# Running sums in 32-column pieces, clamps replaced by a ScalarE test, one test of the last decays, and a written order for the whole kernel

## The chip, the cores and the metric

The kernel runs on one core of one Trainium2 chip. A core has five engines that work side by side, each through its own queue of instructions: TensorE (PE, matrix products, with its weight loads shown apart as PEld), VectorE (DVE), ScalarE (ACT), GpSimd (POOL) and SyncE (SP), which here only issues transfers. The transfers themselves run on 16 DMA engines. The metric is the device time of one execution in microseconds (us).

## What is computed

Two blocks follow each other. The first is a gated linear recurrence with complex decays, over 4 batches, 8 heads, 768 steps and heads of 48 columns. The second is a feed-forward layer with a SoLU activation and a layer norm on 3,072 rows of 384 columns, 1,024 wide inside.

```python
mag = np.sqrt(a_re * a_re + a_im * a_im)
scale = np.minimum(mag, 0.999) / (mag + 1e-06)
a_re_n, a_im_n = (a_re * scale, a_im * scale)
...
for t in range(S):
    ar, ai = (a_re_n[:, :, t, :, None], a_im_n[:, :, t, :, None])
    new_re = ar * S_re - ai * S_im
    new_im = ar * S_im + ai * S_re
    kv = np.einsum('bhd,bhe->bhde', k[:, :, t], v[:, :, t])
    S_re, S_im = (new_re + kv, new_im)
    y[:, :, t] = np.einsum('bhd,bhde->bhe', q[:, :, t], S_re)
...
h = x @ w_in
h_max = np.max(h, axis=-1, keepdims=True)
e = np.exp(h - h_max)
sm = e / (np.sum(e, axis=-1, keepdims=True) + 1e-09)
solu = h * sm
mu = np.mean(solu, axis=-1, keepdims=True)
var = np.mean((solu - mu) ** 2, axis=-1, keepdims=True)
ln = (solu - mu) / np.sqrt(var + 1e-06) * g_ln
return (ln @ w_out).astype(np.float32)
```

Everything is float32 in and out. `w_in`, `w_out` and `g_ln` reach the kernel beside the attention inputs; the wide weights are stored as 64-bit numbers, which the kernel turns into float32 itself.

## The kernel before

The sequence is cut into 6 pieces of 128 steps; with 4 batches that makes 24 **chunks**, numbered by piece and then by batch. Two neighbouring chunks form a **group**, 12 in all. The kernel is a set of named steps, and a written order says which step comes when; a step issues its instructions on whichever engines it uses, and each engine runs its own instructions in that order. Semaphores make an instruction wait for what it reads or overwrites.

For each group, *prep* steps work on tiles of 128 steps x 768 columns: `clamp` bounds a_re from below (L751, which also leaves the largest value in `seen`) and a_im from both sides (L753); `inverse` (ScalarE, Ln and Exp), `ratio` and `tangent` (DVE, L762 to L768) form the tangent of half the angle, the last of them a clamp to 1.5; `square`, `secant`, `fourth`, `size`, `eps`, `lnm` give the logarithm of the bounded magnitude. `total` (L793) multiplies it by a triangle of ones on PE, which is the running sum over 128 steps; `grow` and `decay` (L797, L800) are its exponentials, `ks` and `qs` multiply k and q by them. `angle`, `on`, `phase` (L847, a running sum of the angles), `nearest`, `part`, `cos` and `sin` give the rotation. `trig` and `exp` load ScalarE's function tables. `last` sends the last row of the decays to 16 partitions, `ends` tests it on DVE and copies it twice side by side on POOL, `turn_ends` and `tot` turn it for the state.

For each chunk, `k2` and `q2` (L906) rotate k and q, `kqb` (L915) transposes 32 x 32 blocks on DVE and `kqt0` (L920) finishes the transpose with four transfers on SP. The first two chunks use `kt`, `qt`, `kT`, `qT` on PE and ScalarE instead. `score0` and `score1` (L962) are the products of k and q, `mask0` (L966) cuts them to a triangle, `values` (L994) multiplies by v and by the state, `carry` and `add` update the state. Then the layer: `turned_x`, `up0`, `up1` (L1035), `exp0` (L1045), `solu0` (L1054), `blocks` and `away` (transpose of z, L1072 and L1077), `spread`, `norm`, `centred`, `down0`, `down1` (L1112), `scale` (L1116) and `store` (L1121). Chunks 0, 1, 2 and 23 transpose z on PE with `zt` and `zT`.

The two weight matrices come in 14 pieces. `fetch` (L685) loads a piece as raw 64-bit words, `raised` rounds the low words in two passes on ScalarE (L692, L694), `convert` (L700 to L704) joins high and low on DVE. Later `again` loads each piece a second time and `inspect` (L707) looks for its smallest magnitude. At the end `verdict` (L1139 to L1152) counts all tests; if one of them fails, a general kernel runs afterwards. With the inputs measured here it does not.

PE works in full width for `total` and `phase` (128 output rows at once), and in four pieces of 32 output rows for `up`, `down`, `carry`, `values` and `score`. The order stands in four strings: START for the first chunks, EVEN and ODD, which are used in turn for chunks 2 to 19 with names relative to the chunk (n) or its group (g), and END.

## Time and profile before

| | us |
|---|---|
| median of 3 runs | 436.76 (435.95 to 441.48) |
| the profiled execution, its time | 441.15 |
| the same, span from first to last instruction | 438.4 |
| busy: PE, DVE, ACT, POOL | 392.0, 361.2, 287.2, 51.7 |
| granted TensorE clock, mean | 0.978 of full |

The profile is one execution. A page line of a group gives the code line, the engine, the operation and its tiles, how often it ran, its busy time and the mean duration in ns, and how long the engine had stood idle before it and for whom. Lines with forty digits cut the span in 40 slices of about 11 us, each digit being the busy share in tenths. The chain of waits goes back from the last instruction, at each step to what released it. "SPq" is SP's queue, in which a transfer is issued; "to landing" counts from there.

Some durations that the prediction uses come from the groups with shapes kept apart. Mean ns of one, 128 partitions each:

| line | operation | columns | mean ns | count |
|---|---|---|---|---|
| L751 | a_re clamp with its accumulated value | 768 / 384 | 942 / 548 | 11 / 2 |
| L753 | a_im clamp | 768 / 384 | 554 / 356 | 11 / 2 |
| L768 | tangent clamp | 768 / 384 | 559 / 360 | 11 / 2 |
| L771, L777 | Square on ScalarE | 768 / 384 | 844 and 831 / 507 | 11 / 2 |
| L774 | Ln with a bias on ScalarE | 768 / 384 | 937 / 600 | 11 / 2 |
| L777 | reading ScalarE's accumulated value | 1 | 189 | 13 |
| L692, L694 | the two passes of `raised` | 512 | 760, 723 | 6 |
| L692, L694 | the same | 384 | 649, 615 | 8 |
| L818, L819 | test of the last decays | 48, on 16 partitions | 167, 191 | 12 |
| L822 | POOL copy of the last decays | 96, on 16 partitions | 592 | 10 |
| L830 | copy of the turned decays | 16, on 96 partitions | 170 | 10 |
| L707 | `inspect` | 512 / 384 | 674 / 561 | 6 / 8 |

Transfers, median us to landing: a raw piece of w_in (512 KB) 6.0, of w_out (384 KB) 5.6; f_kqT (192 KB each, four a chunk) 3.4; f_zT (128 KB each) 3.2; an input of a group (384 KB) 4.8 to 5.2; the last decays (3 KB) 3.7; an output (192 KB) 3.8.

### The profile page before, as it was taken

How to read it: one execution, taken by the hardware profiler on the slowest of the kernel's cores; microseconds unless marked ns; L12 is line 12 of the kernel's file. 1: busy time of each engine (PE TensorE's matmuls, PEld its weight loads, DVE VectorE, ACT ScalarE, POOL GpSimd, SP SyncE). 2: the span in 40 equal slices, each digit the busy share in tenths (PEclk: the TensorE clock that was granted, in tenths of full speed). 3: DMA queues.
4: the chain of work that ended last, by engine and by line, in shares of the span. 5: the costliest groups of instructions: out<-in, count | busy, mean ns of one | idle time of the engine just before them, and what ended most of it. 6: DMA issues, size and time to landing. Idle time of an engine off the chain costs nothing.

```text
span 438.4 us, 15186 instructions
## 1 busy us (share of the span) xinstructions
PE 392.0 (89%) x6590; PEld 220.2 (50%) x6590; DVE 361.2 (82%) x540; ACT 287.2 (65%) x453; POOL 51.7 (12%) x149
## 2 busy tenths in 40 slices
PE   0247858999999989999999999999999999999983
PEld 0025333555655545555554554654655646446861
DVE  4798899989889799799899899899899899753230
ACT  3998995986585685585576667668657757703160
POOL 3000011203001100101011011011021021102010
PEclk9985989999999999999999999999999999999999
DMA  8895808678758868989888878789879674473210
GB/s 222 203 261 160 188 9 184 122 180 179 171 113 192 202 145 200 210 175 221 202 187 203 196 181 207 168 206 223 190 177 204 166 157 107 111 191 85 47 38 29
DMA packets 167771, 72.52 MB, mean 165 GB/s; under 512 B 142224, under 2 KB 155536, under 8 KB 167696
## 3 DMA queue, kind: packets, MB, share of 16 engines
q1 hardware_dynamic: 167552, 71.14, 70.5%
q8 instruction: 54, 0.88, 0.9%
q10 hardware_dynamic: 144, 0.33, 0.3%
q14 instruction: 21, 0.17, 0.1%
HBM read 38.87 MB, written 4.72 MB: 99 GB/s over the span
## 4 chain that ended last, share of the span: by engine, by line
PE 73%; DVE 8%; ACT 8%; DMA 5%; issue 3%; SPq 2%; DVEq 0%
PE f_o L1112 26%; PE f_h L1035 22%; PE f_y L994 8%; PE f_score L962 6%; PE f_phase L847 3%; PE f_L L793 3%; PE f_d L1002 3%; DMA f_kqT<-f_kb 3%; DMA f_raw<-in_moe_w_in_dram 2%; SPq L920 1%; ACT f_bits L692 1%; DVE f_kb L915 1%; ACT f_bits L694 1%; DVE f_z L1054 1%; ACT f_kqT L933 1%
## 5 line engine op out<-in xcount | busy, mean ns | idle before, releaser
L1112 PE MATMUL f_o<-f_w_out,f_zT 128*32 128x384 f32 (+1 forms) x1344 | 132.9, 487 | 0.2 <-ACT f_zT L1067 0.2
L1035 PE MATMUL f_h<-f_w_in,f_xT 128*32 128x512 f32 x1152 | 130.4, 593 | 1.1 <-ACT f_xT L1028 1.1
L1112 PEld LDWEIGHTS f_o<-f_w_out,f_zT 128*32 128x32 f32 (+1 forms) x1344 | 60.8, 113 | 56.1 <-issue 46.0
L1035 PEld LDWEIGHTS f_h<-f_w_in,f_xT 128*32 128x32 f32 x1152 | 46.0, 110 | 63.9 <-issue 58.3
L915 DVE STREAM_TRANSPOSE f_kb<-f_kq 128x1536 f32<-128x1536 f32 x22 | 54.3, 2469 | 2.3 <-DMA f_kqT<-f_kb 2.0
L1054 DVE SCALAR_TENSOR_TENSOR f_z<-f_h,f_z 128x1024 f32<-128x1024 f32 (+1 forms) x36 | 33.9, 978 | 22.7 <-ACT f_z L1045 22.7
L1099 POOL TENSOR_SCALAR f_s<-f_s,f_sum 128x1 f32<-128x1 f32 x24 | 8.3, 348 | 272.2 <-ACT f_z L1093 272.1
L962 PEld LDWEIGHTS f_score<-f_kqT 96*32 96x32 f32 x1536 | 33.0, 112 | 14.5 <-issue 9.9
L1116 ACT ACTIVATE f_ot<-f_o,f_rs 128x384 f32<-128x384 f32 x24 | 14.0, 582 | 39.1 <-issue 18.2
L962 PE MATMUL f_score<-f_kqT 96*32 96x64 f32 (+3 forms) x1536 | 35.5, 239 | 4.4 <-DMA f_kqT<-f_kb 1.9
L1045 ACT ACTIVATE f_z<-f_h 128x1024 f32<-128x1024 f32 x24 | 29.3, 1219 | 13.6 <-PE f_h L1035 13.5
L994 PE MATMUL f_y<-f_att,f_vr 128*32 128x128 f32 x384 | 37.0, 273 | 0.0
L994 PE MATMUL f_y<-f_att,f_v 128*32 128x128 f32 (+1 forms) x384 | 36.6, 273 | 0.0
L793 PE MATMUL f_L<-f_lr,f_mats 128*128 128x384 f32 x48 | 20.0, 541 | 17.3 <-DVE f_lr L788 17.3
L994 PE MATMUL f_y<-f_kqT,f_state 96*32 96x128 f32 (+1 forms) x640 | 34.1, 272 | 0.0
L966 DVE TENSOR_TENSOR f_att<-f_score,f_mats 128x1024 f32<-128x1024 f32 x24 | 29.2, 1216 | 2.4 <-PE f_score L962 2.2
L994 PEld LDWEIGHTS f_y<-f_att,f_v 128*32 128x32 f32 (+1 forms) x384 | 22.6, 103 | 10.4 <-issue 7.7
L1093 ACT ACTIVATE f_z<-f_z,f_less 128x1024 f32<-128x1024 f32 x24 | 27.4, 1142 | 0.0
L847 PE MATMUL f_phase<-f_x,f_mats 128*128 128x384 f32 x48 | 20.5, 549 | 6.8 <-ACT f_x L833 6.8
L850 ACT ACTIVATE f_f<-f_phase,f_bias 128x384 f32<-128x384 f32 x24 | 13.9, 579 | 19.4 <-PE f_phase L847 18.5
L1072 DVE STREAM_TRANSPOSE f_zb<-f_z 128x1024 f32<-128x1024 f32 x20 | 24.7, 1236 | 0.3
L906 DVE TENSOR_TENSOR f_kq<-f_cs,f_k 128x768 f32<-128x768 f32 x24 | 22.8, 952 | 2.0 <-ACT f_cs L864 1.2
(104 smaller groups left out, 616.7 us busy)
## 6 DMA issues: line engine op xcount, KB each, us to landing
f_kqT<-f_kb SPq DMA_DIRECT2D x88, 192.0 KB, 3.4
f_zT<-f_zb SPq DMA_DIRECT2D x80, 128.0 KB, 3.2
f_raw<-in_moe_w_in_dram SPq DMA_DIRECT2D x12, 512.0 KB, 6.0
f_raw<-in_moe_w_out_dram SPq DMA_DIRECT2D x16, 384.0 KB, 5.6
f_ar<-in_a_re_dram SPq DMA_DIRECT2D x12, 384.0 KB, 4.8
f_ai<-in_a_im_dram SPq DMA_DIRECT2D x12, 384.0 KB, 4.9
f_q<-in_q_dram SPq DMA_DIRECT2D x12, 384.0 KB, 5.2
f_k<-in_k_dram SPq DMA_DIRECT2D x12, 384.0 KB, 5.1
```

Of the source, the lines that this page charges most:

```text
L793: nc.tensor.matmul(out=ps, lhsT=tri, rhs=st["lr"][:, i * DM:(i + 1) * DM], start=True, stop=True)
L847: nc.tensor.matmul(out=ps, lhsT=turns, rhs=st["x0"][:, i * DM:(i + 1) * DM], start=True, stop=True)
L915: nc.vector.transpose(out=t, in_=T["kq", c].rearrange("p n h (f j) -> p j (n h) f", j=3))
L962: nc.tensor.matmul(out=scores[r0:r0 + 32, x, r:], lhsT=QK[:, r // 32, x], rhs=QK[:, r // 32:, H + x], start=True, stop=True)
L966: nc.vector.tensor_tensor(out=st["att"].rearrange("p (i u) t -> p i u t", u=2), in0=scores.rearrange("p (i u) t -> p i u t", u=2), in1=mat ...
L994: nc.tensor.matmul(**product)
L1035: nc.tensor.matmul(out=st["h"][r:r + 32, half * 512:(half + 1) * 512], lhsT=st["xT"][:, c * P + r:c * P + r + 32], rhs=w_in[:, c, half * 5 ...
L1045: nc.scalar.activation(out=z, in_=h, func=AF.Exp, accum_out=sums[:, n:n + 1])
L1054: nc.vector.scalar_tensor_tensor(out=z, in0=h, scalar=1.0, in1=z, op0=OP.mult, op1=OP.mult, accum_out=st["sum"][:, 2 + i:3 + i])
L1072: nc.vector.transpose(out=st["zb"], in_=st["z"].rearrange("p (c s f) -> p s c f", s=4, f=32))
L1093: nc.scalar.activation(out=st["z"], in_=st["z"], func=AF.Square, bias=st["less"], accum_out=st["sum"][:, 1:2])
L1112: nc.tensor.matmul(out=st["o"][rows], lhsT=zT, rhs=w_out[:, c], start=(c == 0), stop=(c == KF - 1))
```

## The change

Six things change.

1. `total` and `phase` call a helper that multiplies in four pieces of 32 output rows.
2. `clamp` and the clamp of `tangent` are gone. In their place `sure` takes, on ScalarE, the squared distance of a_re x (1 / a_re) from one, and leaves its sum in `seen`; the verdict asks that it be at most 1e-7.
3. `raised` is one pass, with the rounding left to the conversion to integers on output. Its tile has two buffers instead of three.
4. `last` sends the row of decays into one constant tile, twice where it is turned later. The tests of the twelve groups and the POOL copies are gone; the verdict tests all rows at once. `turn_ends` is a product in three pieces, and `tot` a copy on ScalarE instead of DVE.
5. Tiles are allocated where they are first used, so that the two halves of a pair of steps can come in either order.
6. START, EVEN, ODD and END are replaced by one string that names every step. Nearly all steps stand at other places than before.

```diff
-    rawp, bits = pool("f_raw", 6), pool("f_bits", 3)
+    rawp, bits = pool("f_raw", 6), pool("f_bits", 2)
...
+    rows = const.tile([GH, NG, 2, D], FP, name="f_rows")
...
             y = T["bits", i] = bits.tile([P, NW], I32, tag="bits", name="f_bits")[:, 0:n]
-            nc.scalar.activation(out=y.bitcast(FP), in_=T["raw", i][:, :, 0].bitcast(U32), func=AF.Identity,
-                                 scale=2.0 ** -29, bias=magic)
-            nc.scalar.activation(out=y, in_=y.bitcast(FP), func=AF.Identity, bias=mmagic)
+            nc.scalar.activation(out=y, in_=T["raw", i][:, :, 0].bitcast(U32), func=AF.Copy, scale=2.0 ** -29)
...
-            nc.vector.tensor_scalar(out=ar, in0=ar, scalar1=LEAST, scalar2=None, op0=OP.max, op1=OP.max,
-                                    accum_out=seen[:, 1, o:o + 1])
-            nc.vector.tensor_scalar(out=ai, in0=ai, scalar1=1e15, scalar2=-1e15, op0=OP.min, op1=OP.max)
...
+        def sure(cs, o=g):
+            nc.scalar.activation(out=st["u"][:, cs], in_=st["x0"][:, cs], func=AF.Square, bias=mone,
+                                 accum_out=seen[:, 1, o:o + 1])
+
         def tangent(cs):
             ai, x0 = st["ai"][:, cs], st["x0"][:, cs]
             nc.vector.scalar_tensor_tensor(out=x0, in0=x0, scalar=2.0, in1=ai, op0=OP.subtract, op1=OP.mult)
-            nc.vector.tensor_scalar(out=x0, in0=x0, scalar1=1.5, scalar2=-1.5, op0=OP.min, op1=OP.max)
...
+        def running(ps, i, weights, nm):
+            for r in range(0, P, 32):
+                nc.tensor.matmul(out=ps[r:r + 32], lhsT=weights[:, r:r + 32], rhs=st[nm][:, i * DM:(i + 1) * DM],
+                                 start=True, stop=True)
+
         def total(i):
             ps = st["L", i] = ps_t.tile([P, DM], FP, tag="t", padded_shape=[P, 512], name="f_L")
-            nc.tensor.matmul(out=ps, lhsT=tri, rhs=st["lr"][:, i * DM:(i + 1) * DM], start=True, stop=True)
+            running(ps, i, tri, "lr")
...
         def last():
-            st["ends"] = sml.tile([GH, D], FP, tag="ends", name="f_ends")
-            nc.sync.dma_start(out=st["ends"], in_=st["ar"][P - 1:P, :])
+            for u in range(2 if ti < NC - 1 else 1):
+                nc.sync.dma_start(out=rows[:, g, u], in_=st["ar"][P - 1:P, :])
...
-        def ends():
-            e = st["ends"]
-            ok = sml.tile([GH, D], FP, tag="ok", name="f_ok")
-            nc.vector.tensor_scalar(out=ok, in0=e, scalar1=LEAST, scalar2=None, op0=OP.is_ge)
-            nc.vector.tensor_reduce(out=seen[0:GH, 2, g:g + 1], in_=ok, op=OP.add, axis=AX.X)
-            if ti < NC - 1:
-                e2 = st["e2"] = sml.tile([GH, 2, D], FP, tag="e2", name="f_e2")
-                nc.gpsimd.tensor_copy(out=e2, in_=e.unsqueeze(1).to_broadcast([GH, 2, D]))
-
         def turn_ends():
             ps = st["tot"] = ps_t.tile([P, GH], FP, tag="t", padded_shape=[P, 512], name="f_tot")
-            nc.tensor.transpose(out=ps[0:D2], in_=st["e2"].rearrange("p u d -> p (u d)"), identity=ident[0:GH, 0:GH])
+            ends = rows[:, g].rearrange("p u d -> p (u d)")
+            for r in range(0, D2, 32):
+                nc.tensor.matmul(out=ps[r:r + 32, 0:GH], lhsT=ends[:, r:r + 32], rhs=ident[0:GH, 0:GH], start=True, stop=True)
...
-            nc.vector.tensor_copy(out=T["tot", g], in_=st["tot"][0:D2])
+            nc.scalar.copy(out=T["tot", g], in_=st["tot"][0:D2])
...
-            nc.tensor.matmul(out=ps, lhsT=turns, rhs=st["x0"][:, i * DM:(i + 1) * DM], start=True, stop=True)
+            running(ps, i, turns, "x0")
...
+        nc.vector.memset(row[:, 3:4], 0.0)
+        nc.vector.tensor_scalar(out=ends, in0=rows[:, :, 0], scalar1=LEAST, scalar2=None, op0=OP.is_ge, op1=OP.add,
+                                accum_out=row[0:GH, 3:4])
```

Of the order, the beginning of the old START and of the new string, up to the first `total`, and the part of the new one from chunk 2's scores to chunk 3's:

```diff
-load_ar:0 load_ai:0 clampb:0 clampa:0 inverseb:0 fetch:5 ratiob:0 inversea:0 raised:5 tangentb:0 ratioa:0
-tangenta:0 fetch:9 squareb:0 raised:9 secantb:0 squarea:0 fourthb:0 sizeb:0 secanta:0 convert:9 fetch:0 epsb:0
-sizea:0 fetch:13 lnmb:0 epsa:0 lnma:0 raised:0 fourtha:0 convert:0 convert:5 gain:0 fetch:2 total1:0 decay1:0
...
+load_ar:0 inverseb:0 load_ai:0 ratiob:0 inversea:0 ratioa:0 sureb:0 surea:0 fetch:10 raised:10 tangentb:0 squareb:0
+load_q:0 fetch:1 tangenta:0 squarea:0 secantb:0 secanta:0 sizeb:0 fourthb:0 sizea:0 epsb:0 convert:10 fetch:0 epsa:0
+load_k:0 lnmb:0 fetch:3 raised:0 lnma:0 total1:0 fourtha:0 total0:0 decay1:0 grow1:0 convert:0 grow0:0 fetch:4
...
+qs1:1 up1:1 zT0:0 up0:1 last:1 centre:0 tangent:2 score0:2 square:2 score1:2 centre:3 centre:4 secant:2 centre:5 ks1:1
+exp0:1 size:2 load_k:2 centre:1 centre:6 q2:3 eps:2 load_v:1 fourth:2 k2:3 lnm:2 kqb:3 down0:0 turn_ends:1 tot:1
+total0:2 spread:0 total1:2 grow1:2 grow0:2 mask0:2 decay0:2 decay1:2 trig:2 solu0:1 down1:0 angle:2 load_ar:3 values:2
+kqt0:3 norm:0 scale:0 on:2 load_vr:2 load_ai:3 zt0:1 turned_x:2 zt1:1 carry:2 qs0:2 zT0:1 zT1:1 centred:1 phase0:2
+qs1:2 phase1:2 ks1:2 score1:3 load_v:2 score0:3 up1:2 nearest0:2 nearest1:2 ks0:2 part0:2 load_v:4 part1:2 sin:2 add:2
```

In EVEN stood `again:-4`, `again:-3`, `inspect:-5` and `inspect:-6`, so that the second loads ran through the loop. In the new string the first, `again:12`, stands beside chunk 6; the other thirteen and all `inspect` steps come after chunk 22's scores. The end of the old END and of the new string:

```diff
-up0:23 store:20 up1:23 centred:22 blocks:22 scale:21 away:22 exp0:23 solu0:23 spread:22 down0:22 norm:22
-centred:23 down1:22 zt0:23 zt1:23 scale:22 store:22 zT0:23 spread:23 zT1:23 store:21 down0:23 down1:23 norm:23
-scale:23 store:23
...
+centred:22 store:20 blocks:22 up0:23 scale:21 up1:23 spread:22 away:22 again:2 inspect:5 exp0:23 norm:22 inspect:3
+down0:22 again:0 down1:22 solu0:23 inspect:9 centred:23 scale:22 again:11 again:6 zt0:23 zT0:23 inspect:0 inspect:6
+zt1:23 again:4 again:8 store:22 spread:23 inspect:2 store:21 down0:23 norm:23 inspect:8 again:1 zT1:23 down1:23
+inspect:11 inspect:4 scale:23 store:23 inspect:1
```

## The prediction

> **What bounds the kernel now.** I read the page first, then windows along the span, then the chain of waits, then the queues in the places the chain points to.
>
> ```profile
> PE 392.0 (89%) x6590; PEld 220.2 (50%) x6590; DVE 361.2 (82%) x540; ACT 287.2 (65%) x453; POOL 51.7 (12%) x149
> ...
> PE   0247858999999989999999999999999999999983
> ...
> DVE  4798899989889799799899899899899899753230
> ```
>
> TensorE (PE) is saturated from about the seventh slice (11 us each) to the last but one; before that DVE is the full one. So there are three stages: a fill that PE waits through, a loop, a drain.
>
> ```profile
> 22.00:33.00 11.00, 5.06 (x13) 2.44 (x14) 10.53 (x22) 10.59 (x19) 0.44 (x1) 0.87 0.95 262
> ...
> 55.00:66.00 11.00, 6.41 (x102) 3.52 (x102) 10.21 (x25) 10.23 (x18) 1.47 (x4) 0.84 0.04 8
> ...
> 153.50:186.60 33.10, 31.68 (x591) 17.21 (x594) 29.55 (x40) 21.31 (x33) 3.36 (x11) 1.00 0.80 186
> 186.60:217.80 31.20, 31.20 (x588) 17.15 (x588) 29.21 (x40) 21.17 (x33) 4.08 (x11) 1.00 0.89 203
> ...
> 425.00:438.40 13.40, 6.04 (x23) 3.29 (x21) 0.46 (x3) 2.86 (x5) 1.33 (x5) 0.92 0.16 53
> ```
>
> A row gives the stretch, its length, then busy us by engine. In the fill PE works 5 to 9 of 11 us and DVE 10.2 to 10.5: **DVE bounds the fill**. In the loop one pair of chunks takes 31.2 to 31.3 us with PE busy throughout and DVE at 29.2: **PE bounds the loop**. One pair takes 33.1, with 1.4 us of idle PE.
>
> ```profile
> 63.28 0.87 DVE f_ar L751 x2
> 64.14 0.47 DVE f_ai L753
> ...
> 67.35 2.29 DVE f_kb L915
> ...
> 71.65 3.97 DMA f_kqT<-f_kb
> 75.76 1.28 PE f_score L962 x34
> ...
> 302.80 1.49 PE f_L L793 x4
> ...
> 310.16 1.51 PE f_phase L847 x4
> ...
> 319.39 5.16 PE f_o L1112 x64
> ```
>
> This is the chain that ended last (start, length, what). The clamps of L751/L753 stand on it in front of the block transpose of chunk 2 (f_kb); its transfer lands and chunk 2's scores start at 75.76. From there the chain is nearly all matmuls back to back. L793 and L847, the running sums, take 1.49 and 1.51 us a pair; the 64 pieces of f_o take 5.16, that is 0.645 us for each 384-column product over all 128 rows (8 of them).
>
> ```profile
> 169.46 2.86 SPq L685 DMA_DIRECT2D f_raw<-in_moe_w_in_dram  x1
> ...
> 172.84 3.08 SPq L868 DMA_DIRECT2D f_on<-f_f  x1
> 176.02 3.51 SPq L920 DMA_DIRECT2D f_kqT<-f_kb  x4
> ```
>
> SP's queue in the slow pair: the re-read of a weight (L685) holds the queue 2.86 us, f_on another 3.08, and only then the next chunk's transpose leaves. PE's scores wait for it until 183.5.
>
> ```profile
> 425.73 5.43 PE L1112 MATMUL f_o<-f_w_out,f_zT 128*128 128x384 f32 x16 [0.24 <-ACT f_zT L1067]
> ...
> 431.33 0.58 ACT L1116 ACTIVATE f_ot<-f_o,f_rs 128x384 f32<-128x384 f32 x1 [3.96 <-PE f_count L1149]
> 431.50 0.14 DVE L1152 TENSOR_SCALAR flag<-f_total 1x1 int32<-1x1 f32 x1
> ```
>
> The end: the last matmuls stop at 431.16, the flag is written at 431.64, and 6.8 us later the span ends. Flag and last store are equally late here.
>
> **The Trainium skill.** "TensorEngine Tiling (Array Packing)", Key Properties: column tiles run independently, and a change of tiling mode drains the array. The trace agrees in size: a full-width pair costs 1.49 us between 32-column neighbours, against 2 x 0.645 = 1.29 for pieces. "ScalarE: Activation LUTs", What ACT_TABLE_LOAD costs: 280 ns + 0.833 ns an element with a pointer bias, so an estimate of 920 ns for 768 elements; L774 with such a bias took 937, L777 without 831. "DMA: Bandwidth & Descriptors", Queues, rings and completion order: each DMA engine takes descriptors of a ring in order, so a small transfer stands behind large ones issued before it on SP; the 3.08 us of f_on behind the weight agrees.
>
> **The change, part by part** (changes of time; minus is a gain).
>
> 1. *Running sums.* 48 full-width products (12 groups, two of L793, two of L847) become 192 pieces. A group goes from 1.49 + 1.51 to 4 x 0.645 = 2.58, so -0.42. Groups 2 to 11 lie where PE bounds: **-4.2**. Groups 0 and 1 lie in the fill and count there. Bounds: 0 if the drain remains in another form, -5 for all twelve.
>
> 2. *Clamps and end tests on DVE.* Removed up to the end of chunk 2's transpose at 69.6: L751 0.548 x 2 + 0.942 x 2 with 0.08 each to read the sum, L753 0.356 x 2 + 0.554 x 2, L768 0.36 x 2 + 0.559, the end test 0.17 + 0.19, f_tot 0.17; 6.9 us together. 2.7 of it is group 0's, in the first 13 us, where DVE idles for loads and ScalarE anyway. **4.2 us** lie in the stretch DVE fills. In the loop DVE loses 1.58 + 0.56 + 0.36 + 0.17 = 2.7 a pair; that shortens nothing on PE by itself, but removes what made the slow pair late.
>
> 3. *ScalarE.* "raised" loses its second pass: 8 x 0.615 + 6 x 0.723 = 9.3 us, all in the fill. The test "sure" adds 0.60 x 2 + 0.19 x 2 for group 0 and 0.94 + 0.19 for each later group, f_tot about 0.2 (no such copy on ScalarE shown; between DVE's 0.17 and the 0.47 of a 384-column copy). To 69.6 that is 9.3 - 4.2 = 5.1 us less. Group 0 gains directly: Ln starts on the landed a_re instead of behind a clamp, and the first running sum's exponentials need no longer follow a two-pass "raised". Walking the written order with these durations, I put decay1 of group 0 near 17.2 instead of 19.69. The new waits: tangent (DVE) now waits for "sure" (ScalarE), because both use f_x; behind tangent on DVE stand conversions, kq products and masks, for which PE waits in turn. "raised" with two f_bits buffers instead of three waits for a conversion (1.5 to 1.9 us), with exp and the copies of kqT behind it.
>
> Parts 2 and 3 with the new order give **-6** for the start of chunk 2's scores, 75.8 to about 69.7: 4.2 from the DVE stretch, about 2 from the earlier start. PE has the same work ahead of that point in both orders (two chunks through up, chunk 0's z turned). Bounds: -1 (each saved DVE op turns into a wait for ScalarE or a load) and -8.
>
> 4. *Order in the loop.* 13 of the 14 re-reads (again) leave the loop for the drain, so the 2.86 us holds on SP go, and with the lighter DVE the idle 1.4 us of the slow pair and 1 us between 77 and 122. New: chunk 3's scores come ahead of chunk 2's up, with only 12 us of PE work to cover DVE's about 14 before its transpose lands; I charge 1. Input loads are spread singly instead of in clusters; up to ten more 3 KB row transfers (second copy of the last decays) cost 0.55 each on SP and replace a POOL copy of 0.59. Net **-1.5**. Bounds: -3 and +8 (nearly 1 us of idle PE a pair; a new order isn't in this trace, so a loss is not excluded).
>
> 5. *The drain.* 13 re-reads of 384 or 512 KB and all 14 reductions (0.56 or 0.67) now follow chunk 22's scores. DMA was at 22% in 400 to 425, so most fit. The last ones don't: weight 8 waits in its buffer for the reduction of weight 9, which stands behind chunk 23's solu on DVE (done 6.9 before PE's end); weight 1 comes after two stores and the reduction of weight 2, about 4.4 before PE's end. With the row's median landing of 6.0 it lands 1 to 2 after PE's end; reduction 0.67, verdict 0.95 and the count follow, and the flag comes 2.5 later than now. **+2.3**; bounds 0 (DMA nearly empty there, landing in 3 us) and +4.5.
>
> 6. *At nothing:* constants and memsets (0.06 each, under the first load), one verdict test less, an added zero fill.
>
> Sum: -4.2 - 6 - 1.5 + 2.3 = **-9.4 us**. The profiled execution took 441.15 us with a span of 438.4, 4.4 above the median of 436.76; I move the difference over unscaled: 436.76 - 9.4 = **427.4**.
>
> **Rivals.**
> - *The gain stays in the fill or is spent in the drain (change within 2%).* For it: DVE and ScalarE alternate in the fill, so a shorter op can become a wait (ScalarE idles 4.54 us at 69 to 74 for f_x); the late re-read. Against: DVE idles under 1.3 us in each slice from 22 to 66. Then -4.2 - 2 + 0.5 + 3 = -2.7: about 434.
> - *The loop gets a new bound (slower).* Mechanism: each group's tangent holds DVE until "sure" comes up on ScalarE behind an exp of h that itself waits for PE; mask and transpose stand behind it. A pair leaves DVE 30.8 - 25.4 = 5.4 us of slack (29.2 less 2.7 and less about 1.1 of reductions moved out). It passes 2% slower when it eats all the gain and 8.7 more, 18.1 over ten groups, that is when the hold is over 5.4 + 1.8 = 7.2 us in every group. For 9 us of hold: 427.4 + 10 x 3.6 = 463. Against: ScalarE is busy only 21.2 of 31.3.
> - *Pieces are no faster than whole products.* Then the sum is -5.2: 431.6. Against it stand f_o and f_h, which run in just such pieces.
>
> **Numbers.** Forecast 0.70: three quarters of it under 428.0. Within-2% rivals together 0.18. New bound 0.07. Fill better than walked and the late re-read hidden, 0.05: near 421. A measurement of this kernel tells about 2% (8.7 us) from no change. Faster by over 2%: 0.52 + 0.05 = 0.57; slower 0.07; the rest, 0.36, within. The forecast alone spans 421 to 433; the range 419 to 436 also takes in most of the small-gain rivals, and leaves out the new bound and some of the tails.
>
> **What would show it.** L793 and L847 as 128*32 rows near 0.32 us of chain per four records; no DVE rows for the clamps; chunk 2's scores near 69.7; pairs near 30.8 us with PE full; the last reduction after PE's last matmul and the flag near 2.5 us behind PE's end. I am wrong if chunk 2's scores start after 74, if pairs exceed 31.3, or if PE's waits name "sure", f_kqT or f_x in the loop.

## The result, and the profile after

| | before | after |
|---|---|---|
| median, first set (20 runs each) | 437.57 | 433.74 |
| ratio, 95% interval | | 0.990 (0.9874 to 0.9926) |
| median, second set (35 and 6 runs) | 438.45 | 433.07 |
| ratio | | 0.986 (0.9816 to 0.9901) |
| median, third set (19 and 6 runs) | 439.07 | 434.57 |
| ratio | | 0.990 (0.9862 to 0.9935) |
| profiled execution, its time and span | 441.15, 438.4 | 432.79, 430.9 |

The ratios are formed from single runs, without one slow run of the changed kernel, and are not exactly the quotients of these medians.

The change makes the kernel 3.8 to 5.4 us faster; forecast were 9.4. The two profiles that lie beside each other differ by 7.5 us of span, nearly twice the medians: the profile of before was a long execution, that of after a short one. This matters below.

From the page of the changed kernel, busy time by engine, then the slices of PE and DVE:

```profile
PE 383.9 (89%) x6928; PEld 207.5 (48%) x6928; DVE 336.9 (78%) x457; ACT 287.7 (67%) x475; POOL 57.6 (13%) x139
...
PE   0258677999999999999998999999999999999990
...
DVE  3789988997798798599788699789787888872352
```

PE has 8 us less to do than before and DVE 24 less; in the loop DVE's slices now stand mostly at 7 to 9. The same kernel in windows (stretch, length, then busy us and instructions of PE, PEld, DVE, ACT, POOL, then granted clock, DMA share and GB/s): two slices of the fill, an undisturbed pair of chunks, a stretch of a little over a pair in the middle, and the end.

```profile
22.00:33.00 11.00, 5.87 (x32) 3.08 (x24) 9.88 (x17) 9.62 (x17) 0.00 (x0) 1.00 1.02 247
55.00:66.00 11.00, 7.54 (x58) 3.21 (x58) 8.23 (x12) 6.57 (x11) 0.00 (x0) 0.84 0.39 66
115.05:145.72 30.67, 30.67 (x620) 16.01 (x616) 24.93 (x29) 22.23 (x37) 5.08 (x13) 1.00 0.73 167
205.35:239.66 34.31, 32.95 (x682) 18.90 (x678) 27.55 (x32) 22.12 (x36) 5.16 (x14) 1.00 0.81 172
418.00:430.90 12.90, 3.06 (x11) 1.44 (x9) 4.14 (x17) 0.58 (x1) 0.00 (x0) 0.81 0.22 81
```

At 55 to 66 DVE works only 8.2 and ACT 6.6 of 11 us: the fill is no longer DVE's there. A pair takes 30.67 instead of 31.27 with PE full and DVE at 24.9. At 205 to 240 PE stands idle for 1.36 us.

What the scores of chunk 2 now wait for, in ScalarE's and then TensorE's timeline (start, length, what; in brackets how long the engine had stood idle and for whom):

```profile
62.05 0.48 ACT L765 COPY f_meanp<-f_parts 128x384 f32<-128x384 f32 x1 [4.37 <-PE f_parts L760]
62.55 1.28 ACT L936 ACT_TABLE_LOAD   x1
63.84 0.58 ACT L1107 COPY f_zT<-f_zt 128x512 f32<-128x512 f32 x1
64.32 0.85 ACT L798 ACTIVATE f_lr<-f_ar 128x768 f32<-128x768 f32 x1
65.20 0.84 ACT L799 ACTIVATE f_x<-f_lr 128x768 f32<-128x768 f32 x1
65.95 0.46 ACT L1068 COPY f_xT<-f_y 128x384 f32<-128x384 f32 x1
```

```profile
56.97 2.46 PE L760 MATMUL f_parts<-f_w_out,f_gs 128*32 128x384 f32 x8 [2.26 <-DVE f_gs L757]
...
60.40 1.59 PE L760 MATMUL f_parts<-f_w_out,f_gs 128*32 128x384 f32 x8
...
66.47 5.36 PE L1075 MATMUL f_h<-f_w_in,f_xT 128*32 128x512 f32 x48 [1.37 <-ACT f_xT L1068]
71.64 1.31 PE L1001 MATMUL f_score<-f_kqT 96*32 96x128 f32 x64
74.53 2.82 PE L1152 MATMUL f_o<-f_w_out,f_zT 128*128 128x384 f32 x8 [1.57 <-DVE f_w_out L770]
```

DVE finished the block transpose of chunk 2 at 62.78; in the kernel before it was 69.63, so the forecast gain of 6 us would have put it near 63.6. But the scores start at 71.64, because chunk 1's h is ahead of them on PE, and its input f_xT is copied by ScalarE behind the mean of w_out, a table load and group 2's two passes of `inverse`. After the scores f_o waits another 1.57 for the centred w_out.

And the end, in DVE's timeline: the last re-read's reduction, and the flag. PE's last product ends at 420.87.

```profile
418.30 1.60 DVE L749 TENSOR_REDUCE f_least<-f_raw 128x1 f32<-128x384 f32 x3 [2.55 <-DMA f_raw<-in_moe_w_out_dram]
420.79 0.69 DVE L749 TENSOR_REDUCE f_least<-f_raw 128x1 f32<-128x512 f32 x1 [0.88 <-DMA f_raw<-in_moe_w_in_dram]
...
423.67 0.14 DVE L1195 TENSOR_SCALAR flag<-f_total 1x1 int32<-1x1 f32 x1
```

The flag comes 2.9 us behind PE's end; forecast were 2.5.

### The profile page after: what moved, and what is told of

Same layout as the page of the kernel before. It is cut to its first block, busy times and chain, and to the rows that moved or that the text cites. A ratio compares the mean times of both kernels' runs of the same rounds, so it can differ in the third digit from the quotient of the medians.

```text
span 430.9 us, 15839 instructions
## 1 busy us (share of the span) xinstructions
PE 383.9 (89%) x6928; PEld 207.5 (48%) x6928; DVE 336.9 (78%) x457; ACT 287.7 (67%) x475; POOL 57.6 (13%) x139
## 4 chain that ended last, share of the span: by engine, by line
PE 69%; DVE 11%; ACT 7%; DMA 5%; SPq 3%; issue 3%; DVEq 0%; ACTq 0%
PE f_o L1152 24%; PE f_h L1075 22%; PE f_y L1034 8%; PE f_score L1001 4%; PE f_phase L838 3%; PE f_L L838 3%; PE f_d L1042 2%; DMA f_v<-in_v_dram 2%; DVE f_kq L947 2%; DVE f_kb L956 1%; DMA f_ar<-in_a_re_dram 1%; DMA f_raw<-in_moe_w_in_dram 1%; SPq L1117 1%; PE f_parts L760 1%; DMA out_dram<-f_ot 1%
## 5 line engine op out<-in xcount | busy, mean ns | idle before, releaser
L1152 PE MATMUL f_o<-f_w_out,f_zT 128*32 128x384 f32 (+1 forms) x1344 | 130.2, 487 | 3.0 <-DVE f_w_out L770 1.6
L1075 PEld LDWEIGHTS f_h<-f_w_in,f_xT 128*32 128x32 f32 x1152 | 42.1, 110 | 65.4 <-issue 61.4
L956 DVE STREAM_TRANSPOSE f_kb<-f_kq 128x1536 f32<-128x1536 f32 x22 | 57.4, 2609 | 2.7 <-DMA f_kqT<-f_kb 2.4
L1139 POOL TENSOR_SCALAR f_s<-f_s,f_sum 128x1 f32<-128x1 f32 x24 | 12.0, 502 | 173.8 <-ACT f_z L1133 173.7
L838 PE MATMUL f_L<-f_lr,f_mats 128*32 128x384 f32 x192 | 19.3, 517 | 17.4 <-DVE f_lr L833 17.4
L1001 PE MATMUL f_score<-f_kqT 96*32 96x64 f32 (+3 forms) x1536 | 33.0, 234 | 1.0 <-ACT f_kqT L974 1.0
L893 DVE SCALAR_TENSOR_TENSOR f_f<-f_f,f_phase 128x384 f32<-128x384 f32 x24 | 12.9, 553 | 21.3 <-ACT f_f L889 21.0
L1130 POOL TENSOR_SCALAR f_less<-f_sum 128x1 f32<-128x1 f32 x24 | 10.8, 448 | 123.5 <-DVE f_z L1094 123.1
L947 DVE TENSOR_TENSOR f_kq<-f_cs,f_q 128x768 f32<-128x768 f32 x24 | 22.8, 950 | 5.0 <-ACT f_cs L902 4.0
L1156 ACT ACTIVATE f_ot<-f_o,f_rs 128x384 f32<-128x384 f32 x24 | 13.6, 568 | 19.4 <-PE f_o L1152 13.5
L1068 ACT COPY f_xT<-f_y 128x384 f32<-128x384 f32 x24 | 11.2, 469 | 22.6 <-PE f_y L1034 22.6
```

The lines of the kernel that those rows point to most:

```text
L838: nc.tensor.matmul(out=ps[r:r + 32], lhsT=weights[:, r:r + 32], rhs=st[nm][:, i * DM:(i + 1) * DM], start=True, stop=True)
L947: nc.vector.tensor_tensor(out=t, in0=T["cs", g][:, i * H:(i + 1) * H], in1=heads(T[nm, g][:, i]).unsqueeze(2).to_broadcast([P, H, 2, D]), ...
L956: nc.vector.transpose(out=t, in_=T["kq", c].rearrange("p n h (f j) -> p j (n h) f", j=3))
L1001: nc.tensor.matmul(out=scores[r0:r0 + 32, x, r:], lhsT=QK[:, r // 32, x], rhs=QK[:, r // 32:, H + x], start=True, stop=True)
L1075: nc.tensor.matmul(out=st["h"][r:r + 32, half * 512:(half + 1) * 512], lhsT=st["xT"][:, c * P + r:c * P + r + 32], rhs=w_in[:, c, half * 5 ...
L1152: nc.tensor.matmul(out=st["o"][rows], lhsT=zT, rhs=w_out[:, c], start=(c == 0), stop=(c == KF - 1))
```

## The experiments

Comparisons are with the kernel before, run beside it on the same chip. "Scores" is the start of chunk 2's scores, "middle" from there to the end of PE's last f_o, "tail" from there to the end of the span.

### e1: the kernel before again

No edit.

> The kernel before, unchanged, profiled once more. Theory A (the profiled execution that the forecast was built on was itself long: 441.15 against a median of 437.57 over 20): this execution has a span near 435, and the 3 us less are missing at a few places of the fill or as waits of PE in the loop (the pair of 33.1 us at 153 to 186 is then near 31.3, chunk 2's scores start earlier than 75.8). Theory B (the executions all look like that one and the time outside the span differs): span near 438, chunk 2's scores near 75.8, a pair of 33 us again. Ratio 1.00 in both.

Measured: 438.16 us, ratio 0.998 (0.9963 to 1.0006); span 436.6, scores 76.02, middle 353.1 (355.4 in the first profile), tail 7.5. The pair of 33.1 us is not there: all pairs between 121 and 340 take 31.27. So about 2 us of the profile that I predicted from belonged to that one execution, and the gain that I booked for "the slow pair" could not be counted on in a median. What I had read as its cause is in e1 as well: the re-read and f_on hold SP's queue for 2.58 and 2.94 us at 169 to 175, and PE idles only 0.2 us in the whole loop. In the first profile the two waits of PE in the slow pair were these:

```profile
PE f_d L1002 <- issue: 1.2, 1, 1.2
PE f_score L962 <- DMA f_kqT<-f_kb: 0.2, 1, 0.2
```

The longer one stands ahead of f_d at 154.2 to 155.4, 14 us before those holds, and the profile names nothing that it waited for. Only the 0.2 us are a wait for the transpose.

### e2: the running sums in pieces, alone

The kernel before with `running` in `total` and `phase`, nothing else.

```diff
-            nc.tensor.matmul(out=ps, lhsT=tri, rhs=st["lr"][:, i * DM:(i + 1) * DM], start=True, stop=True)
+            running(ps, i, tri, "lr")
```

> The kernel before with only the running sums in four pieces of 32 rows, in the old order. If the term of the forecast holds: pairs of 30.8 instead of 31.3, 10 pairs, so -4 to -5 us, ratio 0.989 to 0.991. Rival (DVE, at 29 of 31 us a pair, takes over as the bound, so that the faster sums turn into waits for the transposes): -1 to -2 us, ratio 0.995 to 0.998, with PE idle in the pairs.

Measured: 435.06 us, ratio 0.9935 (0.9913 to 0.9958), that is -2.8 us. The chain of an undisturbed pair by line, first of e1 (246.52 to 277.79), then of e2 (243.24 to 273.88):

```profile
by line: PE f_o L1112 33.5%; PE f_h L1035 33.0%; PE f_y L994 11.3%; PE f_score L962 7.6%; PE f_phase L847 4.8%; PE f_L L793 4.8%; PE f_d L1002 4.6%; PE f_tot L826 0.5%
```

```profile
by line: PE f_h L1040 33.8%; PE f_o L1117 33.8%; PE f_y L999 11.5%; PE f_score L967 7.5%; PE f_phase L793 4.4%; PE f_d L1007 4.3%; PE f_L L793 4.2%; PE f_tot L831 0.6%
```

Of 31.27 and 30.64 us these are: f_L 1.49 and 1.29, f_phase 1.51 and 1.35, and also f_o 10.46 and 10.34, f_d 1.43 and 1.31, f_score 2.38 and 2.30. The products' own rows give 0.36 of the 0.63 us; the rest is in their neighbours in 32-column mode, most plainly in f_d. **A pair gains 0.63 us, not 0.42.** Ten pairs would give 6.3, an estimate; in the old order PE then idles 2.0 us between 93 and 403 (0.2 in e1), and one pair takes 31.58 without any wait, so that less arrives, 2.8 by the medians.

### e3: all edits in the code, the old order

The changed kernel with the old order; `sure` directly after `ratio`, and some conversions moved up for the two f_bits buffers. Around group 3, for example:

```diff
-clamp:3 ... ratio:3 up0:3 tangent:3
+ratio:3 sure:3 up0:3 tangent:3
```

> All code edits of the change, but the old order: clamps and end tests left out, the test on ScalarE put right after ratio, and five conversions of weights moved ahead so that two buffers are enough. If the written order is what spends the gain: ratio under 0.985 (-6.5 us or more: sums -4.5, lighter DVE and ScalarE in the fill -3 to -6, no cost at the end, flag as before about 7 us from the last product to the end of the span). If the written order is itself what brings the earlier chunk 2: ratio 0.988 to 0.995, chunk 2's scores near 74 to 76, and the tail again near 7.2 us.

Measured: 450.64 us, ratio 1.025 (1.021 to 1.030): **slower by 12 us** by the medians (438.5 before). Scores at 80.9. What DVE and, between 85 and 420, PE waited for (us in total, times, longest):

```profile
DVE f_x L816 <- ACT f_u L811: 13.5, 13, 1.5
```

```profile
PE f_score L1004 <- DMA f_kqT<-f_kb: 4.6, 6, 1.5
PE f_d L1045 <- issue: 3.4, 2, 2.6
```

L816 is `tangent`, L811 `sure`: the hold of my rival "the loop gets a new bound" is there, about 1.1 us a group instead of the 7.2 from which it decides. In the changed kernel's own order the same wait is 0.3 us in all. That this hold makes mask and transpose late, and so PE's waits for f_kqT, is likely, but no run shows it alone. In the fill it is something else: the transpose of chunk 2 ends at 69.7, as in e1 (69.9), and the 4.9 us by which the scores come later stand on PE ahead of chunk 1's h:

```profile
73.55 7.56 PE L1078 MATMUL f_h<-f_w_in,f_xT 128*32 128x512 f32 x48 [4.77 <-ACT f_xT L1071]
```

Here `sure` of group 2, put directly after `ratio`, waits on ScalarE for DVE, and the copy of x for chunk 1 stands behind it. The 7.56 us are a product at half clock for the most part (5.36 in the changed kernel). So the 12 us belong to all the edits with `sure` at this place; another place in the old order was not tried, and the running sums alone pay in it (e2).

### e4: the re-reads in the loop, in the new order

The changed kernel with its 14 `again` and `inspect` steps spread over groups 2 to 11, as in EVEN, for group 4:

```diff
-secant:4 load_vr:3
+secant:4 again:4 load_vr:3
...
-lnm:4 score0:6
+lnm:4 inspect:3 score0:6
```

> The changed kernel with the 14 second loads and their reductions put back through the loop (two a pair, ended by group 9), the rest of its order as it is. If the tail costs what its trace shows: from PE's last product to the end of the span 7.2 instead of 10.0 us, so -2.5 to -3 us against the changed kernel, ratio to before near 0.983. Rival (the loads hold SP's queue and DMA in the loop as before): the tail shrinks by 2.8 but the pairs grow by 0.3 or more, ratio 0.988 to 0.993.

Measured: 435.56 us, ratio 0.9933 (0.99 to 0.9966). The flag comes 0.48 behind PE's end, but the middle is 354.3 in this profile. The executions fall in two groups, 433.3 to 434.7 with a mean granted clock of 0.98 to 0.993, and 435.6 to 438.8 with 0.973 to 0.978; the profile is of the second. So the re-reads in the loop are no gain on the whole, and may be no loss either.

### e5 and e13: the changed kernel again

No edit.

> The changed kernel again, unaltered. If its first profile stands for it, the span is 430 to 433 us, chunk 2's scores start at 71 to 72.5 and the pairs take 30.5 to 30.9. If that execution was a lucky one, the way my base execution was an unlucky one, the loop shows it: more than 352 us from chunk 2's scores to TensorE's last matmul (349.2 in the first profile), and a ratio to the kernel before of 0.992 or more.

> The changed kernel, unaltered, as the base of this call. 432.5 to 434 us as in the two calls before; chunk 2's scores at 71.2 to 72.5, and the pairs of groups 6 and 8 longer than 30.7 by 1 to 2 us together.

Measured: 433.07 and 434.57 us. Against e1, in us:

| | e1 | after | e5 | e13 |
|---|---|---|---|---|
| scores | 76.02 | 71.64 | 71.88 | 71.83 |
| middle | 353.1 | 349.2 | 349.9 | 351.4 |
| tail | 7.5 | 10.0 | 12.6 | 12.3 |
| span | 436.6 | 430.9 | 434.4 | 435.5 |

In these three the start of the scores repeats within 0.3, but that is luck: kernels with the same order up to there have it at 71.2 to 73.5 (e4, e8, e10), and e12 and e14, one kernel, at 73.1 and 69.6. The first profile was short in its tail and middle; those of e5 and e13 are the slowest of their six executions. What PE waited for in e5 between 85 and 420:

```profile
PE f_y L1034 <- DMA f_v<-in_v_dram: 0.6, 1, 0.6
PE f_o L1152 <- ACT f_ot L1156: 0.6, 1, 0.6
PE f_h L1075 <- ACT f_xT L1068: 0.3, 1, 0.3
PE f_o L1152 <- ACT f_zT L1107: 0.3, 1, 0.3
```

Between 93 and 403 PE idles 1.6 to 1.9 us in the three profiles, e1 0.2. The new order costs idle time in the loop where I had booked a gain.

### e6: full-width sums in the new order

```diff
-            running(ps, i, tri, "lr")
+            nc.tensor.matmul(out=ps, lhsT=tri, rhs=st["lr"][:, i * DM:(i + 1) * DM], start=True, stop=True)
```

and the same for `turns`.

> The changed kernel with the running sums as full-width products again. If the pieces are worth in the new order what they were alone in the old one (-2.8 us) or what I forecast (-4.2), this kernel is 2.8 to 4.2 us slower than the changed one, close to the kernel before (ratio 0.997 to 1.0), and pairs take 31.0 to 31.3. If the saving is covered in the new order by waits for other engines, it is under 1.5 us slower.

Measured: 439.79 us, 6.7 above e5 beside it; ratio to before 1.002 (0.9991 to 1.0045). **Without the pieces the whole change is worth nothing.** Its scores start 4.2 us earlier than in e1, but the middle is 1.8 and the tail 4.1 us longer: the gain of the fill is spent behind it. The window of an undisturbed pair of e6:

```profile
146.86:178.13 31.27, 31.27 (x594) 16.08 (x590) 26.10 (x32) 22.09 (x36) 3.73 (x10) 1.00 0.76 157
```

31.27 again, as in the old order, with DVE 3 us lighter: a lighter DVE does nothing for a pair in which PE is full.

### e7 and e16: the fill in another order

e7 is the changed kernel with chunk 1's turned_x ahead of inverse:2 and three centre steps ahead of ratio:2.

```diff
-load_q:3 centre:2 values:1 zT1:0 inverse:2 ratio:2 kqt0:2 centre:7 onward:1 turned_x:1 sure:2
+load_q:3 centre:2 centre:7 centre:0 centre:3 values:1 zT1:0 turned_x:1 inverse:2 ratio:2 kqt0:2 onward:1 sure:2
```

> The changed kernel with chunk 1's turned_x ahead of group 2's inverse on ScalarE, and three of the eight centre steps ahead of group 2's ratio on VectorE. If what kept chunk 2's scores at 71.6 instead of 69.7 is the place of these steps in the written order, the scores start near 70.1, the product f_o after them no longer waits 1.6 us for f_w_out, and the time falls by 1.5 to 3 us against the changed kernel. If the fill is bound elsewhere (the two Exp/Ln passes of group 2 now come 0.5 later, and its tangent with them), the scores move but the time stays within 0.7 us.

Measured: 435.88 us, 2.8 more than e5. Scores at 72.2; up:1 no longer waits for f_xT, but f_o waits longer. PE's timeline at f_o, and windows of e7:

```profile
76.69 3.54 PE L1154 MATMUL f_o<-f_w_out,f_zT 128*128 128x384 f32 x5 [3.16 <-DVE f_w_out L772]
```

```profile
70.00:76.00 6.00, 3.53 (x88) 1.83 (x80) 5.01 (x9) 4.78 (x6) 0.00 (x0) 0.99 0.88 142
76.00:82.00 6.00, 5.31 (x8) 2.52 (x8) 6.00 (x7) 2.93 (x6) 0.00 (x0) 0.50 0.45 60
```

In the 3.2 us of idle PE the clock (third number from the end) falls to 0.50, from 75.8 to 82.7. The Trainium skill, "TensorE: Matmul & The Clock Gate", What's actually happening, says that after an idle window of about 3.4 us, which runs freely, TensorE falls to half rate. The traces agree in kind: each profile of before and after shows half clock somewhere in the fill, for 3.4 us or a multiple of it, and not at the same place in every execution (e1 at 77.3 to 80.7, the first profile of before not there). They differ in one thing: PE need not have idled for all of such a window. In the 3.4 us ahead of these stretches it had idled 1.9 us in e1, 2.3 in e5 and 2.3 in e7. e16 puts repeated products into that gap:

```diff
+            if (c, half) == (2, 1):
+                xs += [0, 1, 2, 3, 4, 5, 6, 7, 0, 1, 2, 3, 4, 5, 6, 7]
+            for x in xs:
```

> The kernel of e7 (turned_x and three centre steps earlier) with all sixteen half-head products of chunk 2's scores formed twice more right after score1:2, about 2.6 us of additional work for TensorE where it idled 3.16 us before f_o and then ran at half clock for six us (74 to 82). If that half clock is what made e7 2.8 us slower than the changed kernel, this kernel has full clock from 74 on and is 2 to 3 us faster than e7's 435.9, near the changed kernel. If not, it is as slow as e7 or slower by the additional work.

Measured: 434.73 us, ratio 0.990 (0.9868 to 0.9936; e7: 0.995, 0.9924 to 0.997, so that the two are only nearly apart); the changed kernel beside it, e13, 434.57. The same two windows of e16:

```profile
70.00:76.00 6.00, 5.10 (x194) 4.33 (x185) 5.63 (x10) 5.74 (x7) 0.00 (x0) 1.00 1.16 176
76.00:82.00 6.00, 6.00 (x58) 2.95 (x60) 6.00 (x10) 5.09 (x11) 1.05 (x3) 1.00 0.25 54
```

The clock stays at 1.00, and the scores start at 69.7, where I had forecast them. Both need care, for e7's profile is the slowest of its 22 executions and e16's the fastest of its 6. Up to the scores the two kernels are the same, and yet e7 has them at 72.2. From the start of f_mean to the scores it takes 7.7 us in both and 9.1 in after and e13: the wait for f_xT was worth 1.3 us, and the rest of e16's early start belongs to its execution. For the clock the other executions speak too: its mean is over 0.984 in none of e7's 22, but in 3 of 6 of e16, 5 of 6 of e5 and 4 of 6 of e13. So work that nobody needs probably removed the half clock. But the total is no better than the changed kernel's: the scores start 2.1 earlier than in e13, the extra products take 2.3, and f_o starts at 74.2 instead of 74.7.

### e15: the same for the gap ahead of the mean

The changed kernel with chunk 1's scores formed once more, and half of them twice more, behind score0:1.

```diff
+            if (c, half) == (1, 0):
+                xs += [4, 5, 6, 7, 0, 1, 2, 3, 4, 5, 6, 7]
```

> The changed kernel with twelve head products of chunk 1's scores formed a second time right after score0:1, the same values into the same place: about 2 us of additional work for TensorE at 54.7 to 56.7, where it idled 2.3 us before the first product of the mean and then ran at half clock. If the idle stretch is what halves the clock, the products of the mean run at full clock (about 1.45 us for each eight instead of 2.46 and 1.59), and chunk 2's scores start no later or up to 1.5 us earlier, though TensorE has 2 us more to do. If the clock falls for another reason, the additional work only adds: scores 0 to 0.5 later, the mean still at half clock.

Measured: 437.63 us, ratio 0.997 (0.9944 to 0.9994), 3 us slower than e13. The clock had already halved at 52.5, behind 2.25 us of idle time ahead of f_phase, so the filler ran slowly; and e13 without it has the mean at full clock as well (1.45 and 1.48). The scores start at 71.74, as in e13. This run tells nothing on the cause. Its loss is in the loop, where PE idles 3.1 us between 93 and 403; why the filler should do that there I can't say.

### e8: the re-reads two places earlier in the drain

Of the end of the order (the first two stand beside chunks 20 and 21):

```diff
-scale:22 again:11 again:6 zt0:23 zT0:23 inspect:0 inspect:6 zt1:23 again:4 again:8 store:22
+scale:22 again:4 again:8 zt0:23 zT0:23 inspect:11 inspect:6 zt1:23 again:1 store:22
```

> The changed kernel with thirteen re-reads and their reductions two places earlier in the drain, each in the place that the one two before it had, the first two beside chunks 20 and 21. If the flag is late only because the last re-read lands late, it comes 0.5 to 1 us behind TensorE's last matmul instead of 2.9, and the time falls by 2 to 2.5 us. If the DMA engines or VectorE's queue are what is full at the end, TensorE ends later by about what the flag gains and the time stays within 0.7 us.

Measured: 432.14 us, 0.9 less than e5, ratio 0.9846 (0.9799 to 0.9893). The flag comes 0.48 behind PE's end, as expected, 3.2 earlier than in e5; but from flag to span end it takes 9.4 us, in the kernel before 6.8. This led to e11.

### e9: the clamps on VectorE in the new order

`clamp` of the kernel before directly ahead of each inverse, the clamp of `tangent` back, no `sure`; the verdict's bound on `seen` is the old one.

```diff
-inverse:3 spread:1 down1:1 turned_x:3 ratio:3 exp0:2 sure:3 solu0:2 kqt0:4 tangent:3
+clamp:3 inverse:3 spread:1 down1:1 turned_x:3 ratio:3 exp0:2 solu0:2 kqt0:4 tangent:3
```

> The changed kernel, order and all, with the three clamps of a group on VectorE again and no ScalarE test. My forecast's term 2 says VectorE's 4.2 us ahead of chunk 2's transpose come back: the transpose ends near 68.5 instead of 64.7, chunk 2's scores start 2 to 4 us later, the loop's pairs stay at 30.7, and the time rises by 3 to 4 us. The rival: in the new order the fill waits for TensorE (the mean of w_out) and ScalarE, so that VectorE's work is hidden, and the time rises by under 1 us; or the clamps also delay the ratio in the loop behind late input loads, and it rises by over 5.

Measured: 460.83 us, ratio 1.053 (1.048 to 1.058), some 27 us above the changed kernel of the other sets: the rival, and far beyond its bound. Waits of DVE, then of PE between 85 and 420:

```profile
DVE f_ar L811 <- DMA f_ar<-in_a_re_dram: 6.5, 3, 3.4
...
DVE f_ai L813 <- DMA f_ai<-in_a_im_dram: 3.3, 4, 1.4
```

```profile
PE f_h L1080 <- DVE f_z L1099: 7.5, 6, 2.0
PE f_zt L1107 <- DVE f_z L1099: 3.7, 2, 3.4
```

At that place DVE waits up to 3.4 us for an input, and solu and the transpose of z stand behind it. So this run gives no price of the clamps; it shows that they can't be put back at this place of the new order, whose loads of a_re come too late for a reader on DVE there. The transpose of chunk 2 ended 2.0 us later than in e5, not 3.8, and the scores started 5.9 us later.

### e10, e11, e12 and e14: three losses taken out

e10 moves two loads of group 7 up.

```diff
-part0:6 nearest1:6 ks0:6 qs1:6 away:9 part1:6 scale:8 onward:6 score0:11 carry:10 sin:6 add:10 cos:6 exp:6 load_ai:7 ks1:6 load_ar:7
+part0:6 load_ar:7 nearest1:6 ks0:6 qs1:6 away:9 part1:6 load_ai:7 scale:8 onward:6 score0:11 carry:10 sin:6 add:10 cos:6 exp:6 ks1:6
```

> The changed kernel with load_ar:7 and load_ai:7 moved ahead of nearest1:6 and scale:8, as far ahead of their inverse as the loads of the groups before and after stand. If the 1.4 us of idle TensorE between 220 and 242 come from a_re of group 7 landing 7 us after its issue, just when its Ln is due, with chunk 11's turned_x queued behind on ScalarE, the two pairs there together take 61.4 instead of 63 and the time falls by 1.2 to 1.8 us. If the store's landing at 232 alone holds TensorE, only 0.6 to 0.8 us goes.

Measured: 433.86 us, ratio 0.9897 (0.9864 to 0.9931), the same as the changed kernel. The wait for the store is gone, but PE now waits 0.9 us for f_zT at 294 and 0.5 at 212: the loss moved.

e11 sends the last decays once and lets POOL make the second copy.

```diff
-            for u in range(2 if ti < NC - 1 else 1):
-                nc.sync.dma_start(out=rows[:, g, u], in_=st["ar"][P - 1:P, :])
+            nc.sync.dma_start(out=rows[:, g, 0], in_=st["ar"][P - 1:P, :])
+
+        def ends():
+            nc.gpsimd.tensor_copy(out=rows[:, g, 1], in_=rows[:, g, 0])
```

> The changed kernel with one transfer of the last decays a group, the second copy made on POOL as in the kernel before: ten transfers fewer in SP's queue. In the changed kernel SP's closing sequence has one pause of 2.0 to 2.4 us (in one profile 1.1) between two of its instructions, in the kernel before none, and it stands at another instruction wherever the count of SP's instructions differs. If the pause belongs to a place in SP's instruction stream that the longer queue has moved into the end, it is gone: flag to span end near 6.8 us instead of 7.1 to 9.4, and the time falls by up to 2 us. If it belongs to the reads outstanding at the end, it stays and the time is the same within 0.7 us.

Measured: 432.69 us, ratio 0.9895 (0.9861 to 0.9929); by the time alone not to be told from the changed kernel. By the trace the first theory holds: no pause, and 6.4 us from flag to span end. Counting SP's recorded instructions shows where the pause stands (the longest gap in its closing sequence behind the branch, from start to start; the count starts at 0):

```
kernel           SP instructions   longest gap       ahead of number
before, e1, e2         470         0.43              469 (its last)
e11                    466         0.43              465 (its last)
e12, e14               465         0.43              464 (its last)
e4                     474         2.12              472
e8                     476         2.31              472
after, e5, e13         477         1.15, 2.33, 2.22  472
e6, e7, e9             477         2.31, 2.11, 2.29  472
e10, e15, e16          477         2.66, 1.30, 0.84  472
e3                     480         2.42              472
```

In all 12 profiles with more than 472 instructions on SP the pause lies ahead of number 472, whatever that instruction is. A block of instructions that is fetched late would look like this; that it is one was not shown. The last packets of the kind "instruction" ahead of SP's going on end 0.3 to 2.5 us before it, so the trace doesn't settle it. The kernel before ends three short of it.

e12 and e14 are one kernel, with the edits of e8, e10 and e11.

> The re-reads two places earlier, the loads of group 7 earlier and one row transfer a group, together. If the three are separate losses: 2.0 (flag at 0.5 instead of 2.9 behind TensorE's end, of which 0.9 was measured alone) + 1.4 + 2.0 = about 3.5 to 5 us less than the changed kernel, near 429. If they overlap or a moved load delays another transfer, the time stays at 431 to 433.

> The combined kernel again, beside the changed one on the same chip. If its three edits are separate losses of the changed kernel (tail 2.4, SP's pause 0 to 2.3, group 7's loads 0.5 to 1), it is 2 to 4 us faster than the changed kernel in this call and under 0.985 of the kernel before. If its 430.4 was a draw of the executions, the two come out within 1 us.

Measured: 430.42 us, ratio 0.9819 (0.9776 to 0.9862), and 430.10, ratio 0.9808 (0.9775 to 0.9841), in the second case 4.5 us less than e13 beside it. PE's waits between 85 and 420 and the end on DVE, of e14:

```profile
PE f_o L1158 <- ACT f_zT L1113: 0.3, 1, 0.3
PE f_y L1040 <- DVE f_k L866: 0.2, 1, 0.2
PE f_d L1048 <- ACT f_xT L1074: 0.2, 1, 0.2
```

```profile
410.70 3.27 DVE L751 TENSOR_REDUCE f_least<-f_raw 128x1 f32<-128x512 f32 x6
...
418.39 0.14 DVE L1201 TENSOR_SCALAR flag<-f_total 1x1 int32<-1x1 f32 x1
```

PE idles 0.55 us between 93 and 403, all reductions are done 4 us before PE's end, and the tail is 7.3 us as before the change. This profile is the fastest of its seven executions, but by the medians too this kernel beats both.

## Why the prediction was wrong

Right in direction, and the measured time lies in the range; wrong in size by about half. The terms of its sum beside what the profiles showed:

| term | forecast | e1 to after | e1 to e5 | e1 to e13 |
|---|---|---|---|---|
| running sums | -4.2 | -6.3 | -6.3 | -6.3 |
| scores of chunk 2 | -6 | -4.4 | -4.1 | -4.2 |
| written order | -1.5 | +2.5 | +3.1 | +4.6 |
| drain, tail | +2.3 | +2.6 | +5.1 | +4.8 |
| sum | -9.4 | -5.6 | -2.2 | -1.1 |

The row of the sums is an estimate, 0.63 x 10 pairs; the row of the written order is the change of the middle less these. 1.6 us of it is f_o's wait behind the scores, 1.4 to 1.7 are additional idle time of PE in the loop. These are single executions; the medians changed by -3.8, -5.4 and -4.5.

1. **The step that failed is part 4, "Order in the loop", -1.5.** It booked idle time of PE as gain, 1.4 us in the slow pair and 1 between 77 and 122, and gave SP's holds as the cause. The idle time belonged to one execution: e1 has 0.2 us in the whole loop, with the same holds, and in the first profile itself 1.2 of the 1.4 us stand 14 us ahead of them. (The 3.08 us of f_on are the time for which its issue held SP, not the time of the transfer.) I moved the sum to the median "over unscaled" with this in it. The loss I had bounded at +8 and set at 1. The runs show 1.6 to 1.9 us of idle PE in the loop instead of 0.2, at the store and the copy of x around 223 to 233 and at the load of v near 300, and pairs over 31.3, the sign that I had named: the two between 176.5 and 239.7 take 63.2 together. The bound held what came; the value did not.
2. **The fill was mis-sized.** DVE's part came about as forecast: the transpose ends at 62.8 to 64.7, against 63.6. I took for granted that PE has the same work ahead of the scores and is ready; in the new order ScalarE's turned_x of chunk 1, behind group 2's inverse and the mean, holds PE, and f_o's wait of 1.57 follows the scores. Without the wait for turned_x the way to the scores is 1.3 us shorter (e7, e16), and yet there is no gain at the end. The first rival's sentence "a shorter op can become a wait" was the better one.
3. **The running sums were too small** in the forecast by a third. I compared the rows of L793 and L847 alone; they gave 0.36 us a pair, and their neighbours, which I had not counted, the rest of the 0.63. On balance they are the whole gain: with full-width sums the changed kernel equals the one before. That they brought 2.1 us more than forecast covered part of the other misses, which was luck.
4. **The tail was about right for the flag** (2.5 forecast, 2.9 to 3.7 measured) and lacked SP's pause (1.15 to 2.3 us in after, e5 and e13). I counted the ten additional row transfers at 0.55 each in the loop, and not what a longer queue does at its end. e14, which takes out the late re-read, the pause and the late loads of group 7, is 4.5 us faster than e13.
5. **"The loop gets a new bound"** did not come in the order that was written; in the old order its mechanism appeared (13.5 us of waits of tangent for sure, e3). "Pieces are no faster" fell in e2 and e6.

Open: e1 ran 3.4 us of its middle at half clock (77.3 to 80.7) and the changed kernel did not, which is worth 1.7 us. With it, 1 to 3 us beyond the terms named above are lost in the changed kernel, most of them in time in which PE counts as busy; e2 has such pairs too (31.58 us without a wait). The granted clock explains little of the spread between executions: of 120 of the kernel before, the 26 with a mean clock under 0.97 have a median of 439.8 us and the others 438.1; in the changed kernel 13 executions at 0.966 to 0.976 and 18 at 0.985 to 0.990 have 433.7 and 433.6.

## What to carry to other kernels

Price an operation in a pipelined stage by the length of the whole stage with and without it, not by its own row: here the neighbours of the full-width products made up two fifths of what the pieces saved. Before a difference is moved from one profile to a median, look for what only that execution has; here one slow pair was worth 2 us. And measure a change of code together with the order written for it: the edits in the old order, placed as in e3, lost 12 us, and the old tests, put into the new one as in e9, 27.

## What was unexpected of the hardware

- SP's instruction number 472 was preceded by a pause of 0.8 to 2.7 us in each of the 12 profiles that had it, at the end of the program where nothing hides it.
- Behind the branch on the flag every engine stands still: in the kernel before, the next instruction of each starts 3.6 to 4.1 us after the start of its branch. In PE's record the branch itself takes 3.8 us, in SP's 0.05 (432.27 and 432.94), and yet SP goes on only at 436.5. This is about half of the 7.3 us of tail there.
- From within a gap of 3.2 us on PE the clock was at half for 6.8 us (e7). With useless products in the gap it was not (e16), in one profile of each.
